# First-pass attention scores as rows: q stationary in four column strips over 512 turned keys, turned to columns once per head

## Chip, cores and metric

The kernel runs on one core of a Trainium2 chip. The time is device microseconds of that core for one launch; lower is better. Each time is of one execution, and medians are over repeated executions.

## The reference

A decode step of a transformer block with adaptive layer norm, and its gradients. There are two sequences (B = 2) of one new token each, width D = 512, H = 32 heads of 128, a key and value cache of 8192 positions a head, and a gated feed-forward part of width 1376. Cut to what bears on the change:

```
q      = (layernorm(x) * (1 + ca) + sa) @ wq            # one row of 128 per sequence and head
scores = q . k_cache * 128 ** -0.5                      # 8192 per head
p      = softmax(scores)
o      = p @ v_cache
x1     = x + ga * (o @ wo);   out = x1 + gb * ffn(layernorm(x1) * (1 + cb) + sb)
```

The outputs are `out` and the gradients of x, k_cache, v_cache, wq, wo, w1, w3, w2, c and w_mod. The caches are 134 MB each in bf16. Their gradients have the same size, and the value cache is read a second time for them (dp = do . v), so that 709 MB move in all.

## The kernel before

**Two passes over heads.** There are 64 heads (sequence and head; `hb(i)`). The first pass (`job_a`) reads K and V of a head and makes the scores, the exponentials E, the output sum and two sums that the gradients need. The second pass (`c_t`, `c_s`, `c_ds`, `c_dv`, `c_dk`) reads V again and writes the gradients of K and V. First come heads 0 to 39 of the first pass; then heads of both passes alternate; then the second pass runs alone, with the weight gradients as small tasks between.

**Tiling of a head.** A head's K is 128 partitions x 64 blocks of 128 dimensions: partition p holds positions 64p to 64p + 63. It comes as two "halves" of 1 MB, and so does V. A ring of 21 such buffers (`halfp`) holds everything large; loads are issued on SP's queue in the order of their need, as far ahead as the ring has free buffers (`pump`), and the gradients are written from the same ring on POOL's queue.

**Slots.** The order of work is written out by hand in slots (`at(slot, place, f)`): within a slot by place, the engines then follow their own program order. A first-pass head takes 8 slots for turning its keys, and later stages overlap with the following heads. For a head that starts in slot s:

- slots s to s + 7, `a_t`: eight keys blocks are turned by TensorE (`transposes`, L366) into a PSUM tile `tp`, which is copied to an SBUF tile `kt` by ACT (L371), or by DVE (L369) for groups 2 and 6. `kt` has a ring of four, `tp` of three.
- slots s + 2 to s + 9, `a_s` (L386): for each turned block one matmul with the block as the stationary operand and q as a single moving column. It writes one column of the score tile `S_ps`, so scores lie as 128 partitions x 64.
- slot s + 10 `a_max` (L390, DVE), s + 11 `a_bias` (L395 on TensorE, L398 on DVE: the largest score, made common to all partitions), s + 12 `a_exp` (L404, ACT).
- slots s + 13, 15, 17, 19, `a_scale`: DVE multiplies K by E into `ek` (L412), a ring of three, and POOL adds E as a column (L414).
- slots s + 15 (= s + MOFF) to s + 22, `a_m` (L427): 64 matmuls with V stationary sum into `M_ps`. In s + 17 `a_kp` (L449) does 16 matmuls with a 32-column stationary operand, four column strips side by side, over K as it lies; every eighth head its rows are copied (L456) and turned to columns by f32 matmuls with `sel` (L463).
- slot s + 23, `a_evac`: ACT copies 128 columns of `M_ps` (L487) and DVE one column (L488, `OK`).

**PSUM.** `tps` has three tiles, `sps` two (`S_ps` and, in the second pass, `DP`; `scr(n)` hands out pieces of the spare right half of the newest one), `mps` two (`M_ps`, and `mtps()` for the projections of the start, for `c_spread` and for the small tasks), `kps` one. Eight banks are taken.

Of the kernel before, what the change touches and what calls it, by code (L numbers as in the profile page):

```python
# [8 lines left out]
BF16 = mybir.dt.bfloat16  # L9
F32 = mybir.dt.float32  # L10
# [7 lines left out]
def kernel(  # L18
# [26 lines left out]
    nc = tc.nc  # L45
    P = 128
    B, Sq, D = A_x.shape
    assert Sq == 1 and B == 2
    _, H, Sk, Dh = A_k_cache.shape
# [3 lines left out]
    NC = D // P  # L53
    KK = Sk // P
    MC = MD // P
# [4 lines left out]
    GRP = 8  # L60
    QK = 16
    assert KK % QK == 0 and NC == 4 and H % 4 == 0
    NG = KK // GRP
    NQ = KK // QK
    LAG = 2
# [6 lines left out]
    def hb(i):  # L72
        return i // H, i % H
# [4 lines left out]
    cst = ctx.enter_context(tc.tile_pool(name="cst", bufs=1))  # L78
# [4 lines left out]
    ekp = ctx.enter_context(tc.tile_pool(name="ekp", bufs=3))  # L83
# [18 lines left out]
    def mtps():  # L102
        return mps.tile([P, 512], F32, name="m_ps", tag="m_ps")

    identb = cst.tile([P, P], BF16, name="identb")
# [9 lines left out]
    NST = 4  # L115
    NR = P // NST
# [4 lines left out]
    nc.vector.tensor_reduce(sel[:], identb[:].rearrange("p (j x) -> p x j", j=NST), AX.X, ALU.add)  # L121
    pz = cst.tile([P, NPG * NR + NR], BF16, name="pz")
    nc.vector.memset(pz[:], 0.0)

    rsum = cst.tile([P, NHD], F32, name="rsum")
    OK = cst.tile([P, NHD, 2], F32, name="OK")
# [60 lines left out]
    NPC = HD // PW  # L187
# [22 lines left out]
    qT_bf = col("qT_bf", H, BF16)  # L210
# [70 lines left out]
    row_to_col(rows_in["dy"], dy_col)  # L281
    silu_grad(sigc, sc_col, dslc, NC)

    def mod_part(m0, m1):
        ps = mtps()
        pv = ps[:, 0:(m1 - m0) * B].rearrange("p (k b) -> p k b", b=B)
        for mc in range(m0, m1):
            for kc in range(NC):
                nc.tensor.matmul(pv[:, mc - m0, :], piece(wm_v, kc, mc),
                                 sc_bf[:, kc, :], start=(kc == 0), stop=(kc == NC - 1))  # L290
        nc.vector.tensor_copy(mod[:, m0:m1, :], pv)

    mod_part(0, 2 * NC)
    nc.vector.scalar_tensor_tensor(h1[:], mod[:, NC:2 * NC, :], 1.0, xn1[:], ALU.add, ALU.mult)
    nc.vector.tensor_add(h1[:], h1[:], mod[:, 0:NC, :])
    nc.vector.tensor_copy(h1_bf[:], h1[:])

    HP = H // NPC

    def q_part(pc):  # L300
        ps = mtps()
        pv = ps[:, 0:HP * B].rearrange("p (k b) -> p k b", b=B)
        for h in range(pc * HP, (pc + 1) * HP):
            for kc in range(NC):
                nc.tensor.matmul(pv[:, h - pc * HP, :], piece(wq_v, kc, h),
                                 h1_bf[:, kc, :], start=(kc == 0), stop=(kc == NC - 1))
        nc.vector.tensor_copy(qT[:, pc * HP:(pc + 1) * HP, :], pv)
        nc.vector.tensor_copy(qT_bf[:, pc * HP:(pc + 1) * HP, :], qT[:, pc * HP:(pc + 1) * HP, :])

    q_part(0)  # L310

    events = {}
    seq = [0]
# [1 line left out]
    def at(slot, place, f):  # L315
        seq[0] += 1
        events.setdefault(slot, []).append((place, seq[0], f))

    now = [0]
    PL_EXP, PL_T, PL_X, PL_S, PL_B, PL_MAX, PL_TT, PL_M, PL_FREE, PL_EV, PL_DS, PL_DK, PL_TASK = range(13)  # L320
# [17 lines left out]
    def head_ps():  # L338
        t = stps()
        cur_ps[:] = [t, now[0], 0]  # L340
        return t

    def scr(n):
        if cur_ps[0] is None or now[0] - cur_ps[1] > 7:
            head_ps()
        if cur_ps[2] + n > 256:
            cur_ps[2] = 0
        o = 256 + cur_ps[2]
        cur_ps[2] += n
        return cur_ps[0][:, o:o + n]  # L350
# [2 lines left out]
        return ap.rearrange("p k (a b) -> p k a b", b=2)  # L353

    S_ps = {}
    M_ps = {}
    E2 = {}
    ek = {}
    kts = {}
    MOFF = NG + LAG + 5  # L360
    HG = NG // 2

    def transposes(block, dve):
# [11 lines left out]

    def a_t(i, g):
        if g == 0:
            S_ps[i] = head_ps()
        kts[(i, g)] = transposes(lambda j: kb_(K, i, g * GRP + j), g in (2, 6))

    def a_s(i, g):
        b, h = hb(i)
        kt = kts.pop((i, g))
        for j in range(GRP):
            cc = g * GRP + j
            nc.tensor.matmul(S_ps[i][:, cc:cc + 1], kt[:, j, :], qT_bf[:, h, b:b + 1], start=True, stop=True)  # L386

    def a_max(i):
        rm = hw.tile([P, 1], BF16, name="rm", tag="rm")
        nc.vector.tensor_reduce(rm[:], S_ps[i][:, 0:KK], AX.X, ALU.max)  # L390
        kts[("rm", i)] = rm

    def a_bias(i):
        s = S_ps[i]
        nc.tensor.matmul(s[:, KK:KK + P], kts.pop(("rm", i))[:].to_broadcast((P, P)), nident[:],  # L395
                         start=True, stop=True)
        nm = hw.tile([P, 1], F32, name="nm", tag="nm")
        nc.vector.tensor_reduce(nm[:], s[:, KK:KK + P], AX.X, ALU.min)  # L398
        kts[("nm", i)] = nm

    def a_exp(i):
        s = S_ps.pop(i)
        t = hw.tile([P, KK, 2], BF16, name="e2", tag="e2", bufs=3)
        nc.scalar.activation(t[:], s[:, 0:KK].unsqueeze(2).to_broadcast((P, KK, 2)), ACT.Exp,  # L404
                             bias=kts.pop(("nm", i))[:], scale=SCL, accum_out=rsum[:, i:i + 1])
        E2[i] = t

    def a_scale(i, q):
        t = ekp.tile([P, QK, 130], BF16, name="ek", tag="ek")
        ks = slice(q * QK, (q + 1) * QK)  # L410
        hf, o = divmod(q * QK, HK)
        nc.vector.tensor_tensor(pair(t[:, :, 0:P]), pair(K[(i, hf)][:, o:o + QK, :]),  # L412
                                E2[i][:, ks, :].unsqueeze(2).to_broadcast((P, QK, P // 2, 2)), ALU.mult)
        nc.gpsimd.tensor_copy(t[:, :, P:P + 1], E2[i][:, ks, 0:1])  # L414
        if q == 0:
            nc.gpsimd.tensor_copy(E["t"][:, i % E["n"], :], E2[i][:, :, 0])
        ek[(i, q)] = t
# [66 lines left out]
    def a_evac(i):  # L484
        m = M_ps.pop(i)
        b, h = hb(i)
        nc.scalar.copy(mstate[b][:, h, :], m[:, 0:P])  # L487
        nc.vector.tensor_copy(OK[:, i, 0:1], m[:, P:P + 1])  # L488

    def job_a(i, s):  # L490
        for g in range(NG):
            at(s + g, PL_T, lambda g=g: a_t(i, g))
            at(s + g + LAG, PL_S, lambda g=g: a_s(i, g))
            at(s + g + MOFF, PL_M, lambda g=g: a_m(i, g))
            at(s + g + MOFF, PL_FREE, lambda g=g: a_free(i, g))
        at(s + NG + LAG, PL_MAX, lambda: a_max(i))
        at(s + NG + LAG + 1, PL_MAX, lambda: a_bias(i))
        at(s + NG + LAG + 2, PL_EXP, lambda: a_exp(i))
        for q in range(NQ):
            at(s + NG + LAG + 3 + 2 * q, PL_TT, lambda q=q: a_scale(i, q))  # L500
        at(s + MOFF, PL_EXP, lambda: a_pz(i))
        at(s + MOFF + 2, PL_T, lambda: a_kp(i))
        at(s + MOFF + 2, PL_FREE, lambda: k_free(i, 0))
        at(s + MOFF + 4, PL_FREE, lambda: k_free(i, 1))
        if i % HPB == HPB - 1:
            at(s + MOFF + 3, PL_EXP, lambda: a_kp_rows(i))
            at(s + MOFF + 4, PL_M, lambda: a_kp_out(i))
        at(s + MOFF + NG, PL_EV, lambda: a_evac(i))

    def take_m(b):  # L510
        mstate[b] = hflat()[:].rearrange("p (i d) -> p i d", d=P)
# [2 lines left out]
    def end_a(s):  # L514
        return s + MOFF + NG

    at(2, PL_X, lambda: q_part(1))
    at(4, PL_X, lambda: q_part(2))
    at(6, PL_X, lambda: q_part(3))

    def mod_rest():
        mod_part(2 * NC, MC)
        release(len(wm_v) + len(wq_v))
        wm_v.clear()
        wq_v.clear()
        pump()
# [552 lines left out]

    def c_spread(n):  # L1080
        b, h = hb(n)
        ps = mtps()[:, 0:2 * P]
        nc.tensor.matmul(ps[:, 0:P], Qr_bf[:, b, h:h + 1].to_broadcast((P, P)), identb[:], start=True, stop=True)
        nc.tensor.matmul(ps[:, P:2 * P], DOr_bf[:, b, h:h + 1].to_broadcast((P, P)), identb[:],
                         start=True, stop=True)
        for k, (nm, bufs) in enumerate((("Qr", 3), ("DOr", 2))):
            t = hw.tile([P, P], BF16, name=nm, tag=nm, bufs=bufs)
            nc.scalar.copy(t[:], ps[:, k * P:(k + 1) * P])
            QD[(n, k)] = t
        e = hw.tile([P, KK, 2], BF16, name="e2", tag="e2", bufs=3)  # L1090
        nc.scalar.copy(e[:], E["t"][:, n % E["n"], :].unsqueeze(2).to_broadcast((P, KK, 2)))
        E2[("c", n)] = e
# [59 lines left out]
    DQ_bf = hcol("DQ_bf", BF16)  # L1152

    def task_dq(b):
        ps = mtps()
        bs = slice(b * H, (b + 1) * H)
        for h in range(H):
            nc.tensor.matmul(ps[:, h:h + 1], mstate[b][:, h, :], DO_bf[:, b, h:h + 1], start=True, stop=True)
        dqf = DQ32[:, b, :]
        kbf = OK[:, bs, 1]  # L1160
        nc.vector.tensor_mul(kbf, OK[:, bs, 1], SIG[:, b, :])
        nc.vector.tensor_tensor(dqf, ps[:, 0:H], kbf, ALU.subtract)
        nc.vector.scalar_tensor_tensor(dqf, dqf, SCL, rtot[:, b, :], ALU.mult, ALU.mult)
        nc.vector.tensor_copy(DQ_bf[:, b, :], DQ32[:, b, :])
        mstate.pop(b)
        release()
        pump()
# [268 lines left out]
```

## Time and profile before

| | |
|---|---|
| median of three runs | 1744.5 us (1744.06 to 1745.21) |
| profiled execution | 1745.59 us, of which the span is 1743.7 us |
| moved by DMA | 709.31 MB, mean 407 GB/s |
| busy: TensorE, its weight loads, DVE, ACT, POOL | 79%, 70%, 66%, 58%, 21% |
| mean granted TensorE clock | 0.797 |

The page's slices are fortieths of the span; a digit is the busy share in tenths. GB/s is what the DMA engines moved in the slice. TensorE's matmuls are pipelined, and their ends are modelled: the busy time of two neighbouring groups overlaps, and what a group costs is better seen from the start of one to the start of the next. A wait line names engine, line and what it waited for, then us in total, the number of times and the longest. A time line row gives start, duration, engine, line, operation, output and inputs, and how many were merged.

### The profile page before, as it was taken

The numbers are of one execution on the slowest core, as the hardware profiler recorded it, in microseconds if no ns is written. First come the engines' busy times: TensorE is split into PE (matmuls) and PEld (weight loads), VectorE is DVE, ScalarE is ACT, GpSimd is POOL, SyncE is SP. The second block draws the span as 40 slices with busy tenths as digits, with TensorE's granted clock in tenths as the row PEclk, the third lists the DMA queues.
The fourth block names the chain that finished last, engine by engine and source line by source line (L and its number), as shares of the span: only waits on it lengthen the run. The fifth ranks groups of instructions, "written<-read, shape, count | busy, mean of one in ns | idle before, by whom it ended". The sixth has DMA issues, their size and how long they took to land. (4 is left out here: it accounts for less than half of the span.)

```text
span 1743.7 us, 54710 instructions
## 1 busy us (share of the span) xinstructions
PE 1370.3 (79%) x24083; PEld 1221.6 (70%) x24083; DVE 1150.4 (66%) x1595; ACT 1008.0 (58%) x1431; POOL 371.9 (21%) x646
## 2 busy tenths in 40 slices
PE   6999999989967787686787778875577776785883
PEld 5999998879867676676776777875455555564672
DVE  2666666867876576577667668785566666675676
ACT  4666666646555545454454555696456555575784
POOL 0333333322221222222122123111011111110111
PEclk9999999989988878887888788698555556566577
DMA  9999999999999999999999999999999999999997
GB/s 381 417 417 418 418 417 389 418 378 398 375 417 422 418 410 422 411 404 414 409 410 412 420 407 394 369 415 420 425 421 421 410 411 395 417 416 415 410 411 319
DMA packets 109402, 709.31 MB, mean 407 GB/s; under 512 B 11175, under 2 KB 17683, under 8 KB 27243
## 3 DMA queue, kind: packets, MB, share of 16 engines
q1 hardware_dynamic: 67280, 421.59, 59.9%
q0 software_dynamic: 36864, 268.45, 37.0%
q10 hardware_dynamic: 5019, 15.78, 2.3%
q8 instruction: 188, 3.08, 0.7%
q14 instruction: 51, 0.42, 0.1%
HBM read 421.57 MB, written 284.20 MB: 405 GB/s over the span
## 5 line engine op out<-in xcount | busy, mean ns | idle before, releaser
L371 ACT COPY kt<-tp 128x1024 bf16<-128x1024 bf16 x794 | 800.9, 1020 | 546.4 <-PE tp L366 536.4
L366 PE MATMUL tp<-identb,half 128*128 128x128 bf16 x8192 | 772.7, 250 | 19.2 <-DVE kt L369 10.6
L366 PEld LDWEIGHTS <-half 128*128 128x128 bf16 x8192 | 599.8, 113 | 107.7 <-issue 94.6
L1106 POOL DMA_DIRECT2D out_dram<-half x256 | 136.2, 532 | 1034.3 <-DVE half L1101 883.0
L427 PE MATMUL m_ps<-ek,half 128*128 128x129 bf16 x4096 | 328.6, 223 | 1.1 <-DMA half<-in_A_v_cache_dram 1.1
L1078 PE MATMUL s_ps<-DO_bf,kt 128*128 128x1 bf16 x4096 | 192.5, 168 | 109.8 <-DVE kt L369 101.8
L1078 PEld LDWEIGHTS <-kt 128*128 128x128 bf16 x4096 | 186.3, 108 | 125.2 <-DVE kt L369 111.8
L369 DVE COPY kt<-tp 128x1024 bf16<-128x1024 bf16 x230 | 157.9, 686 | 153.6 <-PE tp L366 153.1
L386 PE MATMUL s_ps<-qT_bf,kt 128*128 128x1 bf16 x4096 | 177.7, 164 | 101.3 <-DVE kt L369 99.4
L427 PEld LDWEIGHTS <-half 128*128 128x128 bf16 x4096 | 248.9, 98 | 1.4 <-DMA half<-in_A_v_cache_dram 1.2
L386 PEld LDWEIGHTS <-kt 128*128 128x128 bf16 x4096 | 159.7, 98 | 106.2 <-DVE kt L369 103.6
L1230 ACT CAST stg<-m_ps 128x512 bf16<-128x512 f32 (+2 forms) x124 | 72.4, 584 | 68.5 <-PE m_ps L1229 68.4
L449 PE MATMUL k_ps<-half,pz 128*32 128x512 bf16 x1024 | 68.2, 386 | 23.0 <-POOL pz L435 23.0
L1229 PE MATMUL m_ps<-half 2*128 2x512 bf16 (+2 forms) x124 | 73.8, 595 | 1.2 <-ACT half L1204 1.2
L449 PEld LDWEIGHTS <-pz 128*32 128x32 bf16 x1024 | 21.9, 96 | 45.1 <-POOL pz L435 26.0
L1204 ACT CAST half<-m_ps 2x512 bf16<-2x512 f32 (+1 forms) x36 | 19.9, 564 | 34.9 <-PE m_ps L1201 34.4
L398 DVE TENSOR_REDUCE nm<-s_ps 128x1 f32<-128x128 f32 x64 | 18.4, 287 | 19.4 <-PE s_ps L395 19.4
L395 PE MATMUL s_ps<-nident,rm 128*128 128x128 bf16 x64 | 15.5, 243 | 19.4 <-DVE rm L390 19.4
L1312 ACT COPY kt<-tp 128x1024 bf16<-128x1024 bf16 x28 | 30.1, 1081 | 0.2
L1306 PE MATMUL tp<-identb,half 128*128 128x128 bf16 x224 | 20.3, 245 | 4.7 <-ACT kt L371 4.6
L488 DVE COPY OK<-m_ps 128x1 f32<-128x1 f32 x64 | 9.8, 154 | 20.5 <-ACT half L487 18.8
L729 PE MATMUL s_ps<-d_attn_bf,kt 128*128 128x1 bf16 x256 | 11.2, 165 | 14.8 <-ACT kt L718 12.1
(871 smaller groups left out, 1757.9 us busy)
## 6 DMA issues: line engine op xcount, KB each, us to landing
out_dram<-half POOLq DMA_DIRECT2D x256, 1024.0 KB, 13.7
half<-in_A_v_cache_dram SPq DMA_DIRECT2D x252, 1024.0 KB, 12.4
half<-in_A_k_cache_dram SPq DMA_DIRECT2D x128, 1024.0 KB, 19.6
out_dram<-stg ACTq DMA_DIRECT2D x22, 512.0 KB, 10.0
half<-in_A_wq_dram SPq DMA_DIRECT2D x8, 1024.0 KB, 10.2
half<-in_A_wo_dram SPq DMA_DIRECT2D x4, 1024.0 KB, 20.5
half<-in_w_mod_dram SPq DMA_DIRECT2D x3, 1024.0 KB, 15.9
half<-in_B_w_dram SPq DMA_DIRECT2D x3, 1024.0 KB
```

The source lines that it names most:

```text
L366: nc.tensor.transpose(tp[:, j, :], block(j), identb[:])
L369: nc.vector.tensor_copy(kt[:], tp[:])
L371: nc.scalar.copy(kt[:], tp[:])
L386: nc.tensor.matmul(S_ps[i][:, cc:cc + 1], kt[:, j, :], qT_bf[:, h, b:b + 1], start=True, stop=True)
L427: nc.tensor.matmul(m[:, 0:P + 1], vb_(i, kk), t[:, kk % QK, 0:P + 1], start=(kk == 0), stop=(kk == KK - 1), skip_group_check=True)
L449: nc.tensor.matmul(kp["ps"][NR * j:NR * (j + 1), :], pz[:, o:o + NR], K[(i, kk // HK)][:, kk % HK:kk % HK + QP, :], start=False, stop=(h = ...
L1078: nc.tensor.matmul(DP[n][:, cc:cc + 1], kt[:, j, :], DO_bf[:, b, h:h + 1], start=True, stop=True)
L1106: sq_.dma_start(src_of(dst, n)[:, hf * HK:(hf + 1) * HK, :], t[:])
L1229: nc.tensor.matmul(ps[:lw, 0:rw], rsl(ln, lc, lw, step), rsl(rn, rc, rw), start=True, stop=True)
L1230: nc.scalar.copy(st["t"][:lw, o:o + rw], ps[:lw, 0:rw])
L1306: nc.tensor.transpose(tp[:, j, :], rows[kc][:, (m0 + j) * P:(m0 + j + 1) * P], identb[:])
L1312: nc.scalar.copy(kt[:], tp[:])
```

## The change

The scores of the first pass are made the other way round. q is the stationary operand: a 32-column tile in which one column holds q and the others are zero (`qz`, three of them in turn, the column filled by POOL at the head's start; which of the 32 columns holds q is chosen by a shift of the window). The turned keys move, 512 at a time. Four such matmuls go to the four column strips of the array, and so to four groups of 32 PSUM partitions; four rounds fill 16 rows with 512 scores each (`R_ps`, 128 x 512, a tile of `mps`). So `a_s` acts in every second slot, on two groups of turned keys. Then ACT copies the rows to an f32 tile in the ring of `ek` (`a_rows`), and four f32 matmuls with a selection matrix `ssel` turn them to the 128 x 64 columns in `S_ps` that the rest uses (`a_cols`).

Maximum, bias, exponential and scaling come one slot later, and so does `MOFF`. `M_ps` and `R_ps` share the two tiles of `mps`; to this end `a_evac` is a slot earlier relative to `MOFF`, its one-column copy goes from DVE to ACT, and the start's projections, `c_spread` during the first pass and `task_dq` take pieces of `scr` in place of a tile of `mps`.

```diff
+    SW = 512 // P
+    NSL = KK // (SW * NST)
+    SG = SW * NST // GRP
+    ssel = cst.tile([P, NSL * NST], F32, name="ssel")
...
+    NZ = 3
+    qz = [cst.tile([P, NR + NSL - 1], BF16, name=f"qz{k}") for k in range(NZ)]
...
-    MOFF = NG + LAG + 5
+    MOFF = NG + LAG + 6
...
     def a_t(i, g):
         if g == 0:
-            S_ps[i] = head_ps()
+            b, h = hb(i)
+            nc.gpsimd.tensor_copy(qz[i % NZ][:, NSL - 1:NSL], qT_bf[:, h, b:b + 1])
         kts[(i, g)] = transposes(lambda j: kb_(K, i, g * GRP + j), g in (2, 6))
 
     def a_s(i, g):
-        b, h = hb(i)
-        kt = kts.pop((i, g))
-        for j in range(GRP):
-            cc = g * GRP + j
-            nc.tensor.matmul(S_ps[i][:, cc:cc + 1], kt[:, j, :], qT_bf[:, h, b:b + 1], start=True, stop=True)
+        if g % SG < SG - 1:
+            return
+        a = g // SG
+        if a == 0:
+            R_ps[i] = mtps()
+        w = qz[i % NZ][:, NSL - 1 - a:NSL - 1 - a + NR]
+        for j in range(NST):
+            kt = kts[(i, g - SG + 1 + j * SW // GRP)]
+            o = j * SW % GRP
+            nc.tensor.matmul(R_ps[i][NR * j:NR * (j + 1), :], w, kt[:, o:o + SW, :],
+                             start=(a == 0), stop=(a == NSL - 1))
+        for k in range(SG):
+            kts.pop((i, g - k))
+
+    def a_rows(i):
+        t = ekp.tile([P, SW * P], F32, name="srow", tag="ek")
+        nc.scalar.copy(t[:], R_ps.pop(i)[:])
+        kts[("row", i)] = t
+
+    def a_cols(i):
+        S_ps[i] = head_ps()
+        t = kts.pop(("row", i))
+        sv = S_ps[i][:, 0:KK].rearrange("p (m c) -> p c m", c=SW)
+        for c in range(SW):
+            nc.tensor.matmul(sv[:, c, :], t[:, c * P:(c + 1) * P], ssel[:], start=True, stop=True)
...
         nc.scalar.copy(mstate[b][:, h, :], m[:, 0:P])
-        nc.vector.tensor_copy(OK[:, i, 0:1], m[:, P:P + 1])
+        nc.scalar.copy(OK[:, i, 0:1], m[:, P:P + 1])
...
-        at(s + NG + LAG, PL_MAX, lambda: a_max(i))
-        at(s + NG + LAG + 1, PL_MAX, lambda: a_bias(i))
-        at(s + NG + LAG + 2, PL_EXP, lambda: a_exp(i))
+        at(s + NG + LAG, PL_EXP, lambda: a_rows(i))
+        at(s + NG + LAG + 1, PL_EXP, lambda: a_cols(i))
+        at(s + NG + LAG + 1, PL_MAX, lambda: a_max(i))
+        at(s + NG + LAG + 2, PL_MAX, lambda: a_bias(i))
+        at(s + NG + LAG + 3, PL_EXP, lambda: a_exp(i))
         for q in range(NQ):
-            at(s + NG + LAG + 3 + 2 * q, PL_TT, lambda q=q: a_scale(i, q))
+            at(s + NG + LAG + 4 + 2 * q, PL_TT, lambda q=q: a_scale(i, q))
...
-        at(s + MOFF + NG, PL_EV, lambda: a_evac(i))
+        at(s + MOFF + NG - 1, PL_EV, lambda: a_evac(i))
...
     def c_spread(n):
         b, h = hb(n)
-        ps = mtps()[:, 0:2 * P]
+        ps = mtps()[:, 0:2 * P] if now[0] > A_END else scr(2 * P)
```

More of the change, by code (lines that the diff above doesn't have):

```diff
@@ L123 @@
     nc.vector.memset(pz[:], 0.0)
+    SW = 512 // P
+    NSL = KK // (SW * NST)
+    SG = SW * NST // GRP
+    ssel = cst.tile([P, NSL * NST], F32, name="ssel")
+    nc.vector.tensor_copy(ssel[:].rearrange("p (x j) -> p x j", j=NST),
+                          identb[:].rearrange("p (j x) -> p x j", j=NST)[:, 0:NSL, :])
+    NZ = 3
+    qz = [cst.tile([P, NR + NSL - 1], BF16, name=f"qz{k}") for k in range(NZ)]
+    for z in qz:
+        nc.vector.memset(z[:], 0.0)
     rsum = cst.tile([P, NHD], F32, name="rsum")
@@ L282, with mod_part @@
     silu_grad(sigc, sc_col, dslc, NC)
-    def mod_part(m0, m1):
-        ps = mtps()
+    def mod_part(m0, m1, ps):
         pv = ps[:, 0:(m1 - m0) * B].rearrange("p (k b) -> p k b", b=B)
@@ L291, in mod_part @@
         nc.vector.tensor_copy(mod[:, m0:m1, :], pv)
-    mod_part(0, 2 * NC)
+    mod_part(0, 2 * NC, mtps())
     nc.vector.scalar_tensor_tensor(h1[:], mod[:, NC:2 * NC, :], 1.0, xn1[:], ALU.add, ALU.mult)
@@ L298, with q_part @@
     HP = H // NPC
-    def q_part(pc):
-        ps = mtps()
+    def q_part(pc, ps):
         pv = ps[:, 0:HP * B].rearrange("p (k b) -> p k b", b=B)
@@ L308, in q_part @@
         nc.vector.tensor_copy(qT_bf[:, pc * HP:(pc + 1) * HP, :], qT[:, pc * HP:(pc + 1) * HP, :])
-    q_part(0)
+    q_part(0, mtps())
     events = {}
@@ L355 @@
     S_ps = {}
+    R_ps = {}
     M_ps = {}
@@ L515, in end_a @@
         return s + MOFF + NG
-    at(2, PL_X, lambda: q_part(1))
-    at(4, PL_X, lambda: q_part(2))
-    at(6, PL_X, lambda: q_part(3))
+    for pc in range(1, NPC):
+        at(2 * pc, PL_X, lambda pc=pc: q_part(pc, scr(HP * B)))
     def mod_rest():
-        mod_part(2 * NC, MC)
+        mod_part(2 * NC, MC, scr((MC - 2 * NC) * B))
         release(len(wm_v) + len(wq_v))
@@ L1154, in task_dq @@
     def task_dq(b):
-        ps = mtps()
+        ps = scr(H)
         bs = slice(b * H, (b + 1) * H)
```

## The prediction

> **What bounds the kernel now.** I read the page first (span, busy shares, slices, GB/s), then the first pass of batch 0 in four views: busy time by stretch, waits of TensorE and of the load queue, time line.
>
> ```profile
> span 1743.7 us, 54710 instructions
> PE   6999999989967787686787778875577776785883
> DMA  9999999999999999999999999999999999999997
> GB/s 381 417 417 418 418 417 389 418 378 398 375 417 422 418 410 422 411 404 414 409 410 412 420 407 394 369 415 420 425 421 421 410 411 395 417 416 415 410 411 319
> ```
>
> A slice is 43.6 us. The DMA row says that transfers fill the span, so most of the kernel can't gain from an engine. But in slices 2 to 9 TensorE is full as well. By stretches (length, then PE, PEld, DVE, ACT, POOL, clock, DMA share, GB/s):
>
> ```profile
> 87.00:131.00 44.00, 44.00 (x913) 41.05 (x911) 28.68 (x42) 28.66 (x42) 15.96 (x26) 1.00 1.01 418
> 436.00:480.00 44.00, 41.31 (x834) 37.70 (x832) 35.95 (x65) 25.41 (x38) 11.51 (x21) 1.00 0.96 376
> 567.00:610.00 43.00, 30.77 (x581) 28.54 (x581) 25.21 (x30) 23.14 (x32) 10.28 (x17) 0.88 1.01 418
> ```
>
> From about 480 us (one first-pass head in 25.7 us, second-pass heads between) TensorE has a quarter of its time to spare. Before that it has none. Waits from 87 to 262 us:
>
> ```profile
> ACT kt L371 <- PE tp L366: 64.0, 55, 1.5
> PEld L366 <- issue: 7.2, 17, 0.4
> SPq L171 <- DMA half<-in_A_k_cache_dram: 74.4, 34, 3.8
> SPq L177 <- DMA half<-in_A_v_cache_dram: 70.5, 33, 3.6
> ```
>
> The copy engines wait for TensorE; TensorE waits for nobody (the 7.2 us "issue" is 0.42 us once a head). The load queue waits for earlier loads, so the DMA is nearly full too: two limits lie side by side. The per-head minimum (L398) starts at 57.45, 67.53, 77.64, 87.71, 97.78 us: 10.06 us a head, with 10.9 in every eighth. A head's 4.19 MB at 418 GB/s would take 10.03 us. **Anything over some 0.03 us a head that TensorE gains is stopped by the DMA; anything that it loses is paid in full.** A head's stage in the time line:
>
> ```profile
> 154.34 0.27 ACT L487 CAST half<-m_ps 128x128 bf16<-128x128 f32 x1
> 154.50 0.63 PE L427 MATMUL m_ps<-ek,half 128*128 128x129 bf16 x8
> 154.65 0.16 DVE L488 COPY OK<-m_ps 128x1 f32<-128x1 f32 x1 [0.63 <-ACT half L487]
> 155.06 1.05 PE L449 MATMUL k_ps<-half,pz 128*32 128x512 bf16 x16
> 156.04 0.62 PE L366 MATMUL tp<-identb,half 128*128 128x128 bf16 x8
> 156.50 0.34 PE L386 MATMUL s_ps<-qT_bf,kt 128*128 128x1 bf16 x8
> 156.70 0.63 PE L427 MATMUL m_ps<-ek,half 128*128 128x129 bf16 x8
> 156.75 1.01 ACT L371 COPY kt<-tp 128x1024 bf16<-128x1024 bf16 x1 [1.19 <-PE tp L366]
> 157.17 0.61 PE L366 MATMUL tp<-identb,half 128*128 128x128 bf16 x8
> ```
>
> Durations overlap, so costs are read from start to start: turning (T) 0.46, scores (S) 0.20, output (M) 0.47 us a slot. L449 stretches M to the next T from 0.47 to 1.54, so it costs 1.07. Check: 8 x 1.12 + 1.07 + 0.06 (bias) = 10.09.
>
> **What the Trainium skill says.** "TensorE: Matmul & The Clock Gate", section "Wait — 56ns, not 53.3ns?": a matmul of N columns takes N / 2.4 GHz + 2.5 ns from start to start, never under about 25 ns. The trace agrees: T is 0.46 / 8 = 57 ns, S 0.20 / 8 = 25 ns. So the 64 one-column matmuls are far cheaper than their busy time. "TensorEngine Tiling (Array Packing)", section "Key Properties": tiles run independently, but changing the tiling mode drains TensorE. L449 is of the same form as the new scores, and seen in narrow windows its groups of four strips start 0.22 us apart, the last 0.32 before the next T:
>
> ```profile
> 155.06 0.40 PE L449 MATMUL k_ps<-half,pz 128*32 128x512 bf16 x4
> 155.72 0.39 PE L449 MATMUL k_ps<-half,pz 128*32 128x512 bf16 x4
> 156.04 0.23 PE L366 MATMUL tp<-identb,half 128*128 128x128 bf16 x1
> ```
>
> Thus 4 x 0.22 = 0.88 is work and 1.07 - 0.88 = 0.19 the two changes of mode (0.09 going in, 0.10 out).
>
> **The change part by part, for a first-pass head.**
>
> Removed: S in eight slots, 8 x 0.20 = **-1.60 us**.
>
> Added, rows: 16 matmuls of 128x512 in four groups, one group in every other slot between T and M. L449 pays the mode change once for four groups; here each pays it: 0.22 + 0.19 = 0.41, times 4 = **+1.64**. Bounds: 0.22 (changes hidden) gives 0.88; I keep 0.41, since both ends of L449 show the gap.
>
> Added, columns: four f32 matmuls with a 128x128 stationary. The nearest row is L463, four such, once in eight heads (each issued as two):
>
> ```profile
> 118.17 1.01 PE L463 MATMUL s_ps<-sel,kprow 128*128 128x8 f32 x8
> 119.04 0.61 PE L366 MATMUL tp<-identb,half 128*128 128x128 bf16 x8
> ```
>
> Start to start 0.87, and the 10.9 us periods are those heads: **+0.87**. 16 moving columns for 8 should add little; a saving has no reason.
>
> So TensorE issues 1.64 + 0.87 - 1.60 = **+0.91 us** a head, though it has fewer instructions (bounds +0.15 to +0.95).
>
> Moved: the evacuation of M. M and the row scores now share the two m_ps buffers and alternate, so each head's M takes the buffer of the head before. In the built order the first weight load of M waits for ACT, behind one T. Timed from the T of the last slot: that slot is 0.46 + 0.41 + 0.47 = 1.34, the next T ends at 1.80, M is due. ACT's kt copy starts 0.71 after its T (156.04 to 156.75) and ends at 1.72; L487 overlaps it by 0.1 and ends at 1.89; the copy to OK, now on ACT, at some 2.05 (the skill, "ScalarE: Activation LUTs", section "What ACT_TABLE_LOAD costs": 186 ns + 0.833 ns an element, overlapping by 93; the trace has 0.27 for 128 elements, none for one). With a start after the wait M begins near 2.15: **+0.35**. Bounds: 0 (ACT early) and 0.57 (no overlap, slower copy). Behind that M stands all of TensorE's queue.
>
> At no cost, with the cover. ACT gets the row copy (L456's 0.59) and the OK copy, 0.8 us; it is busy 28.7 of 44 us, and the row copy has a slot with L449 before the columns need it; without that cover it is 0.6 at most. DVE loses the 0.16 copy, but its ek products now fall in the slots of its two kt copies: 0.69 + 1.22 = 1.91, in a slot that with L449 lasts 2 us or has a free one after it; else M waits up to 0.5. POOL gets a 128x1 copy (0.25) and is two thirds idle. K is kept a slot longer: a quarter of one of 21 buffers, which are full while TensorE is late. SP's order shifts V by a slot. The second-pass spread moves to the spare half of s_ps, cover three slots behind the reader of DP, in a stage that DMA sets; else some 0.5 us for each of 24 heads. Some 6080 fewer TensorE instructions mean about 0.3 MB less fetched, under 1 us.
>
> Per head 0.91 + 0.35 = **1.26 us**. It counts where TensorE sets the pace: from the second head (47.4 us) to the fortieth (465.6), 38 periods: 48 us. Off this comes what TensorE waits for the DMA there now, since slower work lets the loads arrive first; from 262 to 480 us:
>
> ```profile
> PE s_ps L776 <- DMA half<-in_A_wo_dram: 6.2, 2, 3.6
> PE tp L366 <- DMA half<-in_A_k_cache_dram: 1.6, 2, 1.3
> ```
>
> 48 - 7.8 = **+40 us**. It can't be won back: the DMA is full from 480 us on, and buffers are full at that point already (376 GB/s at 436 to 480 us), so no larger lead is carried over. The profiled execution took 1745.6 us (span 1743.7 and 1.9 around it), 1.1 over the median of 1744.5: 1745.6 + 40 - 1.1 = **1784 us**.
>
> **The rivals.**
> - Forecast, TensorE becomes slower where it has no slack (0.80): 1784, from +0.6 a head (mode change partly hidden, short wait: 23 - 8 = +15, 1760) to +1.48 (56 + a few us where the DVE's dot products share the kt buffers: 1804).
> - Mode changes hidden and the wait covered (0.07): +0.15 a head, 6 us, under the 7.8 that can be taken up: 1744, no change. For it: T's weight loads are otherwise hidden; against it: 0.42 us of idle loads after L449.
> - Not slower, but faster (0.06): the scores cost what their busy time says. The page of 87 to 262 us has 47.0 us in 1096 matmuls, 2.74 us a head; then TensorE gains 0.23 a head, falls to the DMA's pace, and wins what the DMA now lacks at 392 to 480 us: 44 x (1 - 397/417) + 44 x (1 - 376/417) = 6.4, so 1738. It decides if S costs more than 1.64 + 0.87 + 0.35 - 0.2 = 2.66 us a head. Against it: the starts, 0.20 a slot.
> - The mixed stage suffers too (0.07): the spread waits for the DVE, which itself waits for 281 us on output transfers. 24 x 0.5 = 12 us more: 1796; a delay of the reads alone would be hidden.
> - That the four strips run one after the other: 4 x 0.22 more a group, 3 us a head, over 1850. L449 speaks against it; left out.
>
> **How the numbers follow.** Within 0.2% (3.5 us, about what a measurement can tell from no change) is the second case, faster the third; the rest, 0.87, slower. The range 1755 to 1804 leaves out the second and third and a little of the ends.
>
> **What would show it.** Right: L398's period from 10.06 to about 11.3 us, DMA in slices 2 to 8 from 417 to about 370 GB/s, the load queue waiting for TensorE, a new wait of M (its weight load) for ACT's OK copy of 0.3 to 0.4 us a head, four-strip groups with 0.4 us between T and M, columns 0.9, no wait for wo, and the same 25.7 us a pair after 500 us. Wrong: a period of 10.1 (groups at 0.2), or slices 13 to 25 slower.

## The result and the profile after

The changed kernel takes 1782.5 us (median of four, 1782.3 to 1784.2) against 1744.3 us: a ratio of 1.022, 95% interval 1.0203 to 1.0238. Forecast was 1784. The profiled execution took 1782.3 us, span 1780.5. First the page again, with the lines that answer to those of before:

```profile
span 1780.5 us, 49750 instructions
...
PE   6999999999988778787787888787377776785873
...
DMA  9999999995999999999999999999999999999997
GB/s 381 418 417 417 418 376 384 356 371 209 345 374 424 424 424 419 422 413 419 423 410 424 410 422 389 360 387 418 426 421 414 419 406 396 421 409 414 411 414 323
```

There are 5000 instructions fewer, and the span is 37 us longer. The time went where the DMA is no longer full. A slice is now 44.5 us; slices 6 to 12 fall short of 417 GB/s by 504 GB/s together, 504/417 x 44.5 = 54 us of transfer. Before, the shortfall of slices 7 to 11 was 128, or 13 us. The difference of 40 us is about the loss. From slice 13 on the rate is what it was.

The stretches, in the same columns as before:

```profile
87.00:131.00 44.00, 43.66 (x658) 34.78 (x656) 24.76 (x31) 27.53 (x45) 6.58 (x28) 1.00 1.01 417
436.00:480.00 44.00, 42.66 (x621) 33.70 (x619) 32.60 (x59) 26.65 (x42) 8.42 (x23) 0.96 0.78 276
567.00:610.00 43.00, 33.70 (x549) 29.49 (x548) 30.33 (x38) 24.74 (x38) 7.60 (x21) 0.90 1.01 424
```

TensorE is as busy as before in the first stage, with over a quarter fewer matmuls; at 436 to 480 us the DMA share is 0.78 instead of 0.96. The waits from 97 to 290 us, first those of the load queue:

```profile
SPq L181 <- PE m_ps L457: 72.7, 27, 3.3
SPq L187 <- DVE ek L442: 27.8, 24, 1.6
SPq L187 <- PE k_ps L479: 24.7, 14, 1.9
SPq L187 <- DMA half<-in_A_v_cache_dram: 17.1, 8, 3.4
...
PEld L457 <- issue: 18.7, 82, 0.2
```

The load queue now waits for buffers that TensorE holds, where it had waited for earlier loads. TensorE still waits for no other engine by this view. The new "issue" before weight loads of the output (L457) comes 82 times in 17 heads at 0.23 us; in the time line it stands behind each of a head's four row groups, and a fifth time behind ACT's copies of M. A head's maximum (L428) starts every 11.31 us (52.45, 63.76, 75.08, 86.39, 97.70), where it was 10.06, and each eighth period is 12.37:

```profile
152.39 1.01 PE L416 MATMUL s_ps<-ssel,srow 128*128 128x16 f32 x8
...
153.26 0.61 PE L375 MATMUL tp<-identb,half 128*128 128x128 bf16 x8
...
153.79 0.40 PE L401 MATMUL m_ps<-kt,qz_109 128*32 128x512 bf16 x4
...
154.13 0.64 PE L457 MATMUL m_ps<-ek,half 128*128 128x129 bf16 x8
...
156.93 0.61 PE L375 MATMUL tp<-identb,half 128*128 128x128 bf16 x8
...
157.38 0.63 PE L457 MATMUL m_ps<-ek,half 128*128 128x129 bf16 x8
...
158.72 0.64 PE L457 MATMUL m_ps<-ek,half 128*128 128x129 bf16 x8
...
159.20 0.61 PE L375 MATMUL tp<-identb,half 128*128 128x128 bf16 x8
...
159.45 0.27 ACT L517 CAST half<-m_ps 128x128 bf16<-128x128 f32 x1
159.61 0.18 ACT L518 COPY OK<-m_ps 128x1 f32<-128x1 f32 x1
159.86 0.48 PEld L457 LDWEIGHTS <-half 128*128 128x128 bf16 x8 [0.23 <-issue]
159.89 0.63 PE L457 MATMUL m_ps<-ek,half 128*128 128x129 bf16 x8
```

The columns (L416) take 0.87 us up to the next T (L375). A row group (L401) starts 0.53 us after its T (153.26), and the output M (L457) follows 0.34 later: 0.87 instead of the 0.45 in a slot without a group (156.93 to 157.38), so a group costs 0.42. In the last three rows M's first weight load comes 0.07 us after the end of ACT's copy to OK, and M starts 0.69 after its T instead of 0.45: a wait of 0.24 us. The view calls it "issue". The order of the program makes ACT the cause, and an experiment further down tests it.

### The profile page after: what moved, and what is told of

Read it like the earlier page. It is cut to its first block, busy times and chain, and to the rows that moved or that the text cites. A ratio compares the mean times of both kernels' runs of the same rounds, so it can differ in the third digit from the quotient of the medians.

```text
span 1780.5 us, 49750 instructions
## 1 busy us (share of the span) xinstructions
PE 1442.5 (81%) x21523; PEld 1197.8 (67%) x21523; DVE 1149.3 (65%) x1535; ACT 1041.7 (59%) x1559; POOL 249.3 (14%) x710
## 4 chain that ended last, share of the span: by engine, by line
PE 32%; issue 32%; DMA 25%; POOL 5%; DVE 2%; ACT 1%; SPq 1%; POOLq 0%; ACTq 0%; DVEq 0%
DMA half<-in_A_k_cache_dram 15%; PE tp L375 11%; PE m_ps L457 11%; DMA out_dram<-half 6%; POOL out_dram L1137 4%; DMA half<-in_A_v_cache_dram 4%; PE m_ps L401 3%; PE k_ps L479 2%; PE s_ps L416 2%; ACT kt L380 1%; DVE ek L442 1%; DVE half L1132 1%; SPq L165 1%; PE s_ps L1109 0%; SPq L181 0%
## 5 line engine op out<-in xcount | busy, mean ns | idle before, releaser
L375 PE MATMUL tp<-identb,half 128*128 128x128 bf16 x8192 | 748.5, 246 | 77.3 <-DMA half<-in_A_k_cache_dram 66.4
L375 PEld LDWEIGHTS <-half 128*128 128x128 bf16 x8192 | 589.0, 112 | 180.2 <-issue 96.9
L457 PE MATMUL m_ps<-ek,half 128*128 128x129 bf16 x4096 | 342.3, 228 | 8.3 <-DVE ek L442 3.8
L457 PEld LDWEIGHTS <-half 128*128 128x128 bf16 x4096 | 262.6, 101 | 60.5 <-issue 59.5
L1109 PEld LDWEIGHTS <-kt 128*128 128x128 bf16 x4096 | 179.4, 106 | 116.9 <-DVE kt L378 99.0
L416 PE MATMUL s_ps<-ssel,srow 128*128 128x16 f32 x512 | 67.6, 264 | 25.3 <-ACT srow L408 25.2
L416 PEld LDWEIGHTS s_ps<-ssel,srow 128*128 128x128 f32 x512 | 63.5, 195 | 27.7 <-ACT srow L408 27.7
L428 DVE TENSOR_REDUCE nm<-s_ps 128x1 f32<-128x128 f32 x64 | 18.6, 291 | 71.4 <-PE s_ps L425 71.3
L408 ACT COPY srow<-m_ps 128x512 f32<-128x512 f32 x64 | 38.2, 597 | 0.0
L401 PE MATMUL m_ps<-kt,qz_107 128*32 128x512 bf16 x352 | 36.9, 409 | 0.0
L401 PE MATMUL m_ps<-kt,qz_108 128*32 128x512 bf16 x336 | 35.0, 406 | 0.0
L401 PE MATMUL m_ps<-kt,qz_109 128*32 128x512 bf16 x336 | 34.3, 398 | 0.0
```

The source lines that it names most:

```text
L375: nc.tensor.transpose(tp[:, j, :], block(j), identb[:])
L401: nc.tensor.matmul(R_ps[i][NR * j:NR * (j + 1), :], w, kt[:, o:o + SW, :], start=(a == 0), stop=(a == NSL - 1))
L408: nc.scalar.copy(t[:], R_ps.pop(i)[:])
L416: nc.tensor.matmul(sv[:, c, :], t[:, c * P:(c + 1) * P], ssel[:], start=True, stop=True)
L457: nc.tensor.matmul(m[:, 0:P + 1], vb_(i, kk), t[:, kk % QK, 0:P + 1], start=(kk == 0), stop=(kk == KK - 1), skip_group_check=True)
L1109: nc.tensor.matmul(DP[n][:, cc:cc + 1], kt[:, j, :], DO_bf[:, b, h:h + 1], start=True, stop=True)
```

## The experiments

Times are medians, with the ratio to the kernel before and its 95% interval. The kernel before measured 1744.1 to 1744.4 us beside them.

**Is the loss where TensorE has no slack?** Rows for heads 40 to 63 only (`a_t`, `a_rows` and `a_cols` branch in the same way; the later slots and the copies of M on ACT stay for all heads):

```diff
     def a_s(i, g):
+        if not (i >= 40):
+            b, h = hb(i)
+            kt = kts.pop((i, g))
+            for j in range(GRP):
+                cc = g * GRP + j
+                nc.tensor.matmul(S_ps[i][:, cc:cc + 1], kt[:, j, :], qT_bf[:, h, b:b + 1], start=True, stop=True)
+            return
...
```

> The changed kernel, but heads 0 to 39 make their scores as before (one column a matmul, no rows and no turning); heads 40 to 63, which lie between second-pass heads, keep the rows. Theory (the loss is where TensorE sets the pace): period of heads 1 to 39 back at 10.06 us, since M then has both buffers of m_ps and the extra work is gone; total within 3 us of the kernel before, 1742 to 1747. Rival (the spread in s_ps or the longer chain hurts the mixed stage): 10 us or more stay, 1755 or above.

1748.4 us, 1.0024 (1.0011 to 1.0036). The period of the early heads is 10.06 again. So the rows of heads 0 to 39 account for 34 of the 38 us; what is left of the change, with the same matmuls in 24 heads of the mixed stage, adds 4 us. That is a little outside my range. In the profiled execution (span 1750.1) heads 25 to 40 are 4 to 6 us late, head 41 is level with the kernel before, the last first-pass head is 0.8 us late and the end 6.4. So what is left at the end arises after the last row of scores; its cause is open.

**What does the removed part cost?** Scores of the kernel before, twice:

```diff
-            nc.tensor.matmul(S_ps[i][:, cc:cc + 1], kt[:, j, :], qT_bf[:, h, b:b + 1], start=True, stop=True)
+            for _ in range(2):
+                nc.tensor.matmul(S_ps[i][:, cc:cc + 1], kt[:, j, :], qT_bf[:, h, b:b + 1], start=True, stop=True)
```

> The kernel before, with each one-column score matmul done twice (same result). It prices the part that the change removes. Theory (a one-column matmul costs some 25 ns from start to start): 64 x 25 = 1.6 us a head more, period 11.6 to 11.7 us, 38 heads: 61 less the 8 us that now wait for loads, about 1797. Rival (it costs its busy time, 2.74 us a head): period 12.8, about 1840.

1818.6 us, 1.0432 (1.0394 to 1.0469): neither number. Two stretches of its time line:

```profile
151.10 0.54 PE L387 MATMUL s_ps<-qT_bf,kt 128*128 128x1 bf16 x16
151.50 0.63 PE L428 MATMUL m_ps<-ek,half 128*128 128x129 bf16 x8
...
152.82 0.57 PE L428 MATMUL m_ps<-ek,half 128*128 128x129 bf16 x7
153.61 0.22 PE L428 MATMUL m_ps<-ek,half 128*128 128x129 bf16 x1 [0.22 <-issue]
```

Sixteen one-column matmuls take 0.40 us from start to start (151.10 to 151.50), 25 ns each, and the shortest periods are 11.67 us, 1.61 more than before. That is the price of 1.6 us a head. But heads 1 to 24 take 12.8 us in the mean (10.2 before): 1.0 more than that price, and just the rival's number. The trace tells the two apart. The 1.0 us lies in gaps such as the one ahead of the eighth output matmul (153.61; the seven before it started 0.06 apart), and not in what a one-column matmul takes.

The gaps have a pattern. If TensorE's matmuls and weight loads are counted from the start of the trace, late starts (over 0.15 us later than is usual for the same two lines) recur at one place of a count of 256 (remainder 192 to 195). From head 1 to head 24 there are 34 there, 22.9 us together, or 1.0 us a head: the whole excess. Where such a gap inside a group is over 0.3 us, it ends 1.2 to 1.6 us after a packet of 16384 bytes of the instruction queue has landed. So the doubled kernel waits for its instructions, which arrive in blocks of 256. This is read from the trace; no run varies it. In the same heads of the kernel before, the packets land 1.2 to 2.3 us ahead of that place, with three late starts of 0.8 us together; in the changed kernel they land 4.5 to 6.4 us ahead, with none. The busy time of 2.74 us is thus out as a price, and the rival's period came out by chance.

**Is it the issue time of the turning?** Rows and selection in bf16:

```diff
-    ssel = cst.tile([P, NSL * NST], F32, name="ssel")
+    ssel = cst.tile([P, NSL * NST], BF16, name="ssel")
...
-        t = ekp.tile([P, SW * P], F32, name="srow", tag="ek")
+        t = ekp.tile([P, SW * P], BF16, name="srow", tag="ek")
```

> The changed kernel, with the rows copied to bf16 and a bf16 selection matrix, so that the four turning matmuls of a head are bf16 instead of f32 (scores rounded to bf16 before the softmax). Theory (issue time on TensorE): from 0.87 us to about 4 x 0.06 = 0.24 us a head, so the period falls by 0.63 to 10.68 us, and 38 heads save 24 us: about 1758. Rival (the way round through ACT and back costs by its waiting, not by the matmuls' own time): the type changes next to nothing, 1780 or more.

1747.7 us, 1.0018 (1.0011 to 1.0024): 35 us off instead of 24. Part of it is the turning itself:

```profile
153.00 0.25 PE L416 MATMUL s_ps<-ssel,srow 128*128 128x16 bf16 x4
153.11 0.61 PE L375 MATMUL tp<-identb,half 128*128 128x128 bf16 x8
```

0.11 us from start to start, where f32 took 0.87, and the period falls by just that 0.76 to 10.55 us. That would be 38 x 0.76 = 29 if every period fell so; e10 shows that some don't. The way through ACT is the same, so it was hidden, as reckoned. The other 6 us show in the page's rate: 424 to 425 GB/s in slices 2 to 6, where the kernels before and after had 417 to 418 in slices 2 to 5. The smaller `ssel` had moved all later tiles by 32 bytes, so that the ring of large buffers began at byte 32768 of a partition instead of 32800 (32448 in the kernel before).

**Is it the place of the ring?** The same with 32 unused bytes, and the kernel before and the changed one with the ring at 32768:

```diff
+    cst.tile([P, 16], BF16, name="pad")      # in e10; 160 in e9; 32 and NZ = 2 in e11
     rsum = cst.tile([P, NHD], F32, name="rsum")
```

> e3_bf16_cols with an unused tile of 32 bytes a partition, so that the ring begins at 32800 as in the changed kernel. Theory (two effects in e3): the period of a head stays 10.55 us, the reads fall to 417 GB/s, and 38 x 0.76 = 29 us come off the changed kernel: 1753 to 1757. Rival (the place of the ring does nothing): 1747, as e3.

> The kernel before with an unused tile of 320 bytes a partition ahead of the ring, so that the 1 MB buffers begin at byte 32768 of a partition instead of 32448; nothing else changes. In e3_bf16_cols, where the tiles happened to be smaller by 32 bytes and the ring began at 32768, the trace had 424 to 425 GB/s in the reads of the first 260 us against 417 in all others. Theory (the ring's place sets the rate of the loads): 425 GB/s there, TensorE still at 10.06 us a head up to 480 us, and after that some 1% off the mixed stage and less off the rest: 1732 to 1739. Rival (the rate differed for another reason, and the bf16 matmuls alone gave e3 its gain): 1744, 417 GB/s.

> The changed kernel with two q tiles in turn instead of three and a small unused tile, so that the ring begins at 32768. Theory (TensorE sets the pace up to 480 us, the DMA afterwards): the period stays 11.31 us, so the first stage gains nothing from faster loads; the mixed stage gains as in e3, 5 to 10 us: 1772 to 1777. Rival (the place does nothing): 1782; rival (the first stage is the DMA's after all): it would gain there too, 2% of 440 us more, below 1768.

| kernel | us | ratio to before | period of a head | GB/s in slices 2 to 4 |
|---|---|---|---|---|
| bf16 turning, ring at 32800 (e10) | 1752.7 | 1.0050 (1.0035 to 1.0065) | 10.55 | 417, 417, 416 |
| before, ring at 32768 (e9) | 1735.4 | 0.9947 (0.9931 to 0.9964) | 10.06 | 423, 424, 424 |
| changed, ring at 32768 (e11) | 1776.8 | 1.0185 (1.0170 to 1.0201) | 11.31 | 425, 425, 424 |

Shifted back, the rate is 417 again, and the period stays 10.55: up to head 24 a period pays the turning's 0.76 us in full. The time is 29.8 us under the changed kernel's, which looks like 38 x 0.76 = 29 but is not that sum. In the profiled executions, whose spans are 28.5 us apart, e10 is 3.1 us ahead of the changed kernel at head 1, gains 23.6 us from there to head 39, and 1.8 after it. In six of the heads 26 to 32 its period is only 0.29 us shorter, because the bias matmul (L426, which shares the largest score among the partitions) now waits for DVE's row maximum (306 to 383 us):

```profile
PEld L426 <- DVE rm L421: 2.8, 6, 0.5
```

The other direction: with loads faster by 1.7% the period doesn't shorten in e9 or e11 (10.06 and 11.31 stay), so TensorE sets it. The gain of 6 to 9 us comes from waits for loads and from later stages. The unused bytes move the smaller tiles behind them too; that the ring is what counts is argued from the loads being written into it. e9's rate line, for the place alone:

```profile
GB/s 391 423 424 424 424 423 380 421 397 409 364 415 411 421 419 421 416 408 411 417 416 416 408 410 402 374 416 424 426 417 420 414 414 397 420 416 409 414 416 312
```

**Is the change of tiling mode real?** The last row group directly ahead of the key sum:

```diff
-            at(s + g + LAG, PL_S, lambda g=g: a_s(i, g))
+            at(s + g + LAG + (g == NG - 1), PL_S if g < NG - 1 else PL_EXP, lambda g=g: a_s(i, g))
...
-        at(s + NG + LAG, PL_EXP, lambda: a_rows(i))
+        at(s + NG + LAG, PL_X, lambda: a_rows(i))
```

> The changed kernel, with the last of a head's four row groups moved one slot later, directly ahead of the 16 four-strip matmuls of the key sum (the copy of the rows follows it in the same slot). Theory (a change of tiling mode costs 0.19 us, paid by each group that stands alone): one change in and out less, the period falls by about 0.19 to 11.12 us, 38 heads save 7 us: about 1775. Rival (the 0.41 us of a group is the matmuls' own time): no saving, 1782; the later row copy could add up to 0.3 us a head of waiting at the columns, 1782 to 1793.

1773.4 us, 1.0161 (1.0146 to 1.0176), 9 us off; period 11.09, 0.22 less:

```profile
158.41 0.63 PE L457 MATMUL m_ps<-ek,half 128*128 128x129 bf16 x8
158.97 0.40 PE L401 MATMUL m_ps<-kt,qz 128*32 128x512 bf16 x4
159.19 1.04 PE L479 MATMUL k_ps<-half,pz 128*32 128x512 bf16 x16
160.16 0.62 PE L375 MATMUL tp<-identb,half 128*128 128x128 bf16 x8
```

The group next to others of its mode takes 0.22 us. The same matmuls, standing alone, took 0.42. So 0.20 us is paid once for a run of four-strip matmuls and not by each group, which is what the prediction calls the change of mode. What it consists of is not separated: behind each group that stands alone, M's weight loads also sit idle for 0.23 us.

**And the wait of M for its evacuation?** The OK copy back on DVE:

```diff
-        nc.scalar.copy(OK[:, i, 0:1], m[:, P:P + 1])
+        nc.vector.tensor_copy(OK[:, i, 0:1], m[:, P:P + 1])
```

> The changed kernel, with the one-column copy of M to OK back on DVE. Theory (in the first-pass stage every 0.1 us a head on TensorE is paid in full, and M waits 0.24 us a head for ACT's two copies): DVE copies while ACT does its 0.27 us, so the first weight load of M waits for one copy only; the way from T to that M falls from 0.69 to about 0.55 us, the period of a head from 11.31 to about 11.18, and 38 heads save 4 to 5 us: about 1778. Rival (the loss is in the mixed stage, or the wait hides beside another): no change, 1782.

1790.8 us, 1.0261 (1.0244 to 1.0278): 8 us slower than the changed kernel, where I expected 4 to 5 faster.

```profile
160.14 0.61 PE L375 MATMUL tp<-identb,half 128*128 128x128 bf16 x8
...
160.40 0.27 ACT L517 CAST half<-m_ps 128x128 bf16<-128x128 f32 x1
160.70 0.16 DVE L518 COPY OK<-m_ps 128x1 f32<-128x1 f32 x1 [0.36 <-ACT half L517]
...
161.01 0.63 PE L457 MATMUL m_ps<-ek,half 128*128 128x129 bf16 x8 [0.26 <-DVE OK L518]
```

My error: the two copies don't run side by side. DVE's starts when ACT's has ended, as the row of the kernel before that the prediction shows already said ("0.63 <-ACT half L487"). On ACT the second copy overlaps the first; on DVE it comes after it, with a crossing between engines. M starts 0.87 us after its T, 0.18 later, and the period is 11.48, 0.17 longer: 38 x 0.17 = 6.5 of the 8 us. As a test of the mechanism it serves: when the copy ends later, M starts later, and the period grows by as much.

**Versions that might be faster.** All repairs of the rows together; the control for the buffer that they need; and the better of the two kernels with its own turning in bf16:

```diff
-        if g % SG < SG - 1:                       # e13: two groups at a time
+        if g % (2 * SG) < 2 * SG - 1:
...
-    NHALF = 21                                    # e13 and e14
+    NHALF = 20
...
-        t = ktp.tile([P, QP * P], F32, name="kprow", tag="kt")     # e12; sel too
+        t = ktp.tile([P, QP * P], BF16, name="kprow", tag="kt")
```

> The changed kernel with all repairs that the runs point to: bf16 rows and selection, the four row groups in two pairs, the second pair directly ahead of the key sum's matmuls, the ring at 32768; for this the small ring of turned keys has eight tiles and the large ring 20 buffers instead of 21. Theory (prices of the runs): 11.31 - 0.76 (bf16) - 0.22 (next to the key sum) - 0.38 (two changes of mode less) = 9.95 us a head, 0.1 less than before; with the loads at 425 GB/s the stage ends 4 us before e9's, less what one buffer is worth: 1731 to 1740. Rival (pairs do not save the change of mode): 10.3 us a head, about 10 us more: 1745 to 1748.

> e9_before_aligned with 20 large buffers instead of 21: what one buffer is worth, as the control for e13_rows_all. Theory (buffers are full where TensorE sets the pace, and the mixed stage waits for writes anyway): within 4 us of e9, 1735 to 1739. Rival (the mixed stage lives on the lead that the buffers hold): 10 us or more, 1745 and above.

> The kernel before with the ring at byte 32768 (as in e9_before_aligned) and its own turning of key sums (once in eight heads) in bf16 instead of f32 (the sums are rounded to bf16). A try for a faster version. Theory (TensorE sets the pace of the first stage, f32 turning costs 0.87 us and bf16 0.11): every eighth period falls from 10.94 to 10.18 us, five of them by 480 us, 3 to 4 us off e9: about 1732. Rival (with faster loads the stage still gains nothing): 1735, as e9.

e14: 1737.0 us, 0.9961 (0.9947 to 0.9975); one buffer is worth nothing that could be told. e12: 1735.4 us, 0.9949 (0.9932 to 0.9965), the same as e9; every eighth period fell only from 10.94 to 10.90. TensorE's saving of 0.76 us there turned into a wait:

```profile
117.06 0.61 PE L368 MATMUL tp<-identb,half 128*128 128x128 bf16 x8
...
118.03 0.16 DVE L468 COPY OK<-s_ps 128x8 f32<-128x8 f32 x1
...
118.24 0.34 PE L388 MATMUL s_ps<-qT_bf,kt 128*128 128x1 bf16 x8 [0.57 <-DVE OK L468]
```

The next scores come 1.18 us after their T, where they otherwise come 0.44 to 0.46 after it. They wait for DVE's copy of the turned sums, which stands behind a product for `ek`.

e13: 1757.4 us, 1.0071 (1.0051 to 1.0090), over both of its expectations, with a period of 10.62 instead of 9.95. The pairs did save their changes of mode, but two waits grew:

```profile
155.83 0.10 PEld L425 LDWEIGHTS <-rm 128*128 128x128 bf16 x1 [0.30 <-DVE rm L420]
...
156.91 0.62 PE L401 MATMUL m_ps<-kt,qz 128*32 128x512 bf16 x8
...
157.46 0.64 PE L457 MATMUL m_ps<-ek,half 128*128 128x129 bf16 x8
...
159.77 0.61 PE L375 MATMUL tp<-identb,half 128*128 128x128 bf16 x8
...
160.62 0.18 ACT L518 COPY OK<-m_ps 128x1 f32<-128x1 f32 x1
...
160.90 0.63 PE L457 MATMUL m_ps<-ek,half 128*128 128x129 bf16 x8 [0.52 <-ACT OK L518]
```

M comes 1.13 us after its T, where the changed kernel had 0.69. Only these 0.44 us are new, since the 9.95 still held the old wait of 0.24. Another 0.30 is a wait of the bias matmul (L425) for DVE's row maximum. Together they are 0.74, a little over the miss of 0.67. That the row groups in these slots had given ACT and DVE the time for this work is read from the time line and not tested. So of the versions tried none with rows beats the kernel before, and that kernel with its ring at another place, e9, beats both.

## Why the prediction was right

The mechanism was right part by part, and one of its terms was too large. That the total came so close is in part luck, as the count of the stage shows.

- **The bound.** TensorE at 10.06 and the DMA at 10.03 us a head lie side by side. That TensorE sets the period is shown by e9 (loads faster, period the same) and e10 (0.76 us less on TensorE, 0.76 less a period up to head 24); e4 shows that the loss lies in this stage.
- **Scores -1.60.** e7: 25 ns a matmul, 1.61 a head where no instructions are waited for. The third rival, which took the busy time, is out. Its own gain of 0.23 us a head had also left out the wait of 0.35.
- **Rows +1.64.** Four times 0.42. e8 shows the part that is the change of mode; the second rival, 0.22 a group, is what a group costs only next to its like.
- **Columns +0.87.** 0.87 in the trace, and e10 takes just that (less bf16's 0.11) away from a period.
- **Wait +0.35.** The right mechanism, too large by 0.11. Most of this is a slip in the sum: by the duration and the overlap that the prediction itself names, the OK copy ends at 1.98, not at 2.05, and the wait is 0.28. In the trace the copy ends 0.07 us after ACT's first one. The parts sum to 1.68 + 0.87 - 1.60 + 0.24 = 1.19 of the 1.25 that the period grew; 0.06 has no place.
- **The stage.** Here two misses cancel. The forecast counts 38 like periods from head 1 to head 39, 48 us, less 7.8 us of waits for the DMA: 40. In the trace the changed kernel is already 5.1 us late at head 1, 3.0 of them at head 0, which was not reckoned. From head 1 to head 39 it loses only 35.5 us. Heads 27 to 32 grow by 0.8 to 0.9 us each and not by 1.25, since they took 10.4 to 10.7 before, and every eighth period grows by 1.44. Between heads 32 and 33 the delay falls from 39.2 to 34.2, where before TensorE waited for wo; its loads now land in 8.3 us instead of 20.5. So head 39 is 5.1 + 35.5 = 40.6 us late. That this is the forecast's 40 is luck.
- **Not won back.** From head 39 to the end the delay went from 40.6 to 37 us.
- **DMA rate.** Wrong in its place: slices 2 to 5 stayed at 417 to 418, the fall came at slice 6. The loads first ran ahead until the ring was full: (417 - 371) GB/s over 180 us is 8.3 MB, eight buffers. I had taken the rate for a sign of the stage's pace; the period and the load queue's waits are the sign. Nor is slice 10, at 209, the pace of a head: there the load queue stands still once for 17.9 us, until a step of TensorE that prepares the second pass (400 to 446 us):

```profile
SPq L181 <- PE rows L928: 17.9, 1, 17.9
```

- **The mixed stage.** e4 as a whole is 4 us over the kernel before, so nothing shows the fourth rival's 12 us.
- **Slips that decided nothing.** TensorE has 5120 instructions fewer, not 6080; the instruction queues moved 3.16 MB for 3.50, so the 0.3 MB hold. Four strips one after the other would take 3 x 0.22 more a group, 2.6 us a head.

## What to carry to other kernels

Price instructions on TensorE from start to start in the stage where they stand, not from busy time or number. Here 64 one-column matmuls (1.60 us) cost no more than 16 wide ones in four groups that each pay a change of tiling mode (1.68), and the wide ones then need their result turned (0.87). Where two limits lie side by side, a trade on one engine has little to win and much to lose. Set each later gain on it (bf16, grouping) against what it covered: in e10, e12 and e13 part of the time that TensorE saved came back as a wait for DVE or ACT. If the DMA is a limit, look also at where its buffers lie.

## What the runs showed of the hardware that I had not expected

- The place of the 1 MB buffers in a partition goes with the rate of loads: 423 to 425 GB/s from 32768 (six kernels), 416 to 418 from 32448 and 32800 (seven kernels), in slices 2 and 3. All buffers of a kernel have the same remainder by 512 (0 against 192 and 32). Which alignment is the one that counts was not tried.
- Four f32 matmuls with 128x128 stationary and 16 columns take 0.87 us, the same in bf16 0.11: eight times less.
- With twice the one-column matmuls, TensorE runs short of instructions (e7): late starts at one place of every 256 of its instructions, 1.2 to 1.6 us after a 16 KB packet of the instruction queue has landed, 1.0 us a head.
